# Softmax sums by 128x32 column tiles in one PSUM bank, spread by DMA, in a Linformer attention and max-out feed-forward kernel

## The chip, the cores and the metric

The kernel runs on one core of a Trainium2 chip. A core has a matrix engine (TensorE, PE in the profile), a vector engine (VectorE, DVE), a scalar engine for activations (ScalarE, ACT), GpSimd (POOL) and a sync engine (SP). Each takes its own instructions in order and waits on semaphores for the others. DMA transfers are issued from the queues of SP, POOL or ACT. TensorE writes to PSUM, which is used here as 8 banks of 128 partitions x 512 floats. The metric is the device time of one execution in microseconds; a kernel's time is the median of its runs.

## The reference

Batch 8, 8 heads, sequence 1024, head size 64, projection 64. The keys and values of each head are projected along the sequence, attention runs over the 64 projected rows, and the result goes through three parallel linear layers, of which the largest is kept, and an output layer.

```python
k_proj = np.einsum('ks,bhsd->bhkd', E, k)
v_proj = np.einsum('ks,bhsd->bhkd', F, v)
scores = scale * np.matmul(q, k_proj.transpose(0, 1, 3, 2))
scores = scores - np.max(scores, axis=-1, keepdims=True)
attn = np.exp(scores)
attn = attn / (np.sum(attn, axis=-1, keepdims=True) + 1e-09)
attn_out = np.matmul(attn, v_proj)
x = attn_out.transpose(0, 2, 1, 3).reshape(B * S, H * D)   # (8192, 512)
h = np.maximum(np.maximum(x @ w1, x @ w2), x @ w3)         # (8192, 768)
out = (h @ w_out).astype(np.float32)                       # (8192, 512)
```

The inputs are normal draws, q, k and v times 0.1.

## The kernel before

All matmuls are in bf16 with float sums. The feed-forward part of batch b and the attention of batch n = b + 1 are interleaved by hand on TensorE. The main loop goes over the batch steps b = 0 to 7, in each over two chunks of 512 tokens (`ch` 0 and 1), and in each chunk over ten steps. Steps 0 to 5 are `up` (one of six blocks of 128 hidden units): 3 weights x 4 matmuls of 128x512, a ScalarE copy of the first result (`h1s`, L566), and two VectorE maxima (`m12`, L570, and `hT`, L518). Steps 6 to 9 are `down` (one of four output steps of 128 tokens): 6 matmuls of 128x512, a copy to `o_sb` (L613 by L99, on ScalarE from batch step 1 on), and a store on SP's queue after every second one. The first `up` step of a chunk takes the last quarter of its input (`ct` 3) behind all else, so that the last head pair of `xT` may come late.

`plan(b)` says which pieces of attention follow which step. A key (ch, step) names the place: (1, 6) is behind the first output step of the second chunk. `behind` calls these pieces, and their instructions stand in each engine's queue in just that order; nothing reorders them. The pieces:

- `ld(b)` loads q, k, v of a batch from POOL's queue, cast to bf16 on the way. `k_t` and `v_t` have one buffer each, so a load waits until the projection has read the batch before.
- `qd(b)` is the turn of q: four VectorE copies to `q_p`, then a transposing DMA on SP's queue.
- `kproj`, `vproj`, `kt`: projections of k and v (128x64 tiles, L286) with their copies (v's by ScalarE, then by VectorE), and the turn of the projected k.
- `sc(b, g)`: scores of head pair g, four 64x64-tile matmuls into two banks (L202), and, later, the ScalarE exp to `pT` (L213). The exp is not emitted at once: `later` holds it until behind the next `h1s` or `o_sb` copy.
- `za(b, g)`: sums (L222 with `ones`) and values (L222 with `vp`), each four 64x64-tile matmuls into two banks by `pair_mm`. The matrix of ones puts the sum of the 64 exps into all 64 rows of a head, so that it stands beside the values. ScalarE takes the reciprocal as exp(-ln) in two passes (L235, L241) and VectorE multiplies (`scale_x`, L252), which gives `xT`.

Banks are dealt out when the program is built: `two()` takes the aligned pair, and `bank()` the one bank, that is free earliest by a rough clock in the program. On the chip an instruction of TensorE waits until the last reader of its bank is done, and all that stands behind it on TensorE waits too.

For batches 1 to 7 the pieces `sc` and `za` are spread over a batch step one pair at a time. Batch 0 has its own code, by half chunks, in front.

Of the kernel before, what the change touches and what calls it, by code (L numbers as in the profile page):

```python
# [8 lines left out]
FP32 = mybir.dt.float32  # L9
# [6 lines left out]
def kernel(  # L16
# [13 lines left out]
    nc = tc.nc  # L30
# [19 lines left out]
    const = ctx.enter_context(tc.tile_pool(name="const", bufs=1))  # L50
    loads = ctx.enter_context(tc.tile_pool(name="loads", bufs=1))
    att = ctx.enter_context(tc.tile_pool(name="att", bufs=2))
    psum = ctx.enter_context(tc.tile_pool(name="psum", bufs=1, space=bass.MemoryType.PSUM))

    ET = mybir.EngineType
# [23 lines left out]
    def bank():  # L79
        n = min(range(8), key=lambda n: free[n])  # L80
        deal((n,))
        return psum_t[:, n, :], (n,)
# [34 lines left out]

    ident = const.tile([P, P], BF16, name="ident")
    ones = const.tile([P, HALF], BF16, name="ones")
    warm = const.tile([P, 512], BF16, name="warm")  # L120
    warm_f = const.tile([P, 512], FP32, name="warm_f")
    w_sb = [const.tile([P, NCT, DF], BF16, name=f"w{i}_sb") for i in range(3)]
# [10 lines left out]
    def load_tiles(b):  # L133
        qkv[b] = tuple(
            loads.tile([P, H, SI, D], BF16, name=nm, bufs=n)
            for nm, n in (("q_t", 2), ("k_t", 1), ("v_t", 1))
        )
        return qkv[b]
# [33 lines left out]
    nc.vector.memset(warm, 0.0)  # L172
    make_identity(nc, ident)
    nc.vector.memset(ones, 1.0)

    load_w(0, slice(0, 2))
    load_kv(2, V2)
# [7 lines left out]
    load_w(2, slice(2, 4))  # L185
    nc.gpsimd.dma_start(out=wout_sb, in_=moe_w_out.rearrange("(jt p) m -> p jt m", p=P))

    def load(b):
        tiles = load_tiles(b)
        for i in range(3):  # L190
            dma = nc.gpsimd.dma_start(out=tiles[i], in_=view((q, k, v)[i], b))  # L191
            if i == 0 and b - 1 in last_T:
                after(dma, last_T[b - 1])
# [15 lines left out]

    def exps(b, g, lo, nsi, sc):  # L210
        t, ns, ready = sc
        pTs[b, g, lo] = att.tile([P, 2, CHUNK], BF16, name="pT", bufs=4)[:, :, 0:nsi * HALF]
        nc.scalar.activation(out=pTs[b, g, lo], in_=t, func=AF.Exp, scale=scale)  # L213
        runs("s", ready, 0.17 + nsi * 0.107, ns)

# [13 lines left out]
    def sums(b, g, lo, nsi):  # L229
        return pair_mm(b, g, lo, nsi, lambda rows, hp: ones[rows])  # L230

    def invert(b, g, lo, nsi, z):
        t, ns, ready = z
        zl = att.tile([P, 2, CHUNK], FP32, name="zl", bufs=1)[:, :, 0:nsi * HALF]
        nc.scalar.activation(out=zl, in_=t, func=AF.Ln)  # L235
        runs("s", ready, 0.17 + nsi * 0.107, ns)
        if nsi == SI:
            zi = att.tile([P, 2, CHUNK], FP32, name="zi", bufs=2)
        else:
            zi = att.tile([P, 2, CHUNK // 2], FP32, name="zi0", bufs=4)  # L240
        nc.scalar.activation(out=zi, in_=zl, func=AF.Exp, scale=-1.0)  # L241
        zis[b, g, lo] = zi, runs("s", ready, 0.17 + nsi * 0.107)
# [19 lines left out]
            f()  # L262
        later.clear()

    def sc(b, g, lo=0, nsi=SI):
        def f():
            t = scores(b, g, lo, nsi)
            later.append(lambda: exps(b, g, lo, nsi, t))
        return f

    def za(b, g, lo=0, nsi=SI, then=False):
        def f():
            z = sums(b, g, lo, nsi)
            av = values(b, g, lo, nsi)
            invert(b, g, lo, nsi, z)
            if then:
                later.append(lambda: scale_x(b, g, lo, nsi, av))
            else:
                scale_x(b, g, lo, nsi, av)
        return f  # L280
# [40 lines left out]
    def qd(b, parts=1):  # L321

        def f():
            q_p = att.tile([P, NPAIR, SI, 2, D], BF16, name="q_p", bufs=1)
            qTs[b] = att.tile([P, NPAIR * SI, P], BF16, name="qT")
            n = NPAIR // parts
            for lo in range(0, NPAIR, n):
                for g in range(lo, lo + n):
                    copy(
                        "v", q_p[:, g].rearrange("p si h d -> p h si d"),  # L330
                        qkv[b][0][:, 2 * g:2 * g + 2], (), 0.43,
                    )
                last_T[b] = nc.sync.dma_start_transpose(
                    out=qTs[b][:, lo * SI:(lo + n) * SI, :],
                    in_=q_p[:, lo:lo + n].rearrange("p g si h d -> p (g si h d)"),
                )
        return f

    kps = {}
    def kproj(b):  # L340
        def f():
            t, ns = bank()
            proj(b, 1, t, (LO, HI), 4 * D)
            kps[b] = att.tile([P, 2, 2 * D], BF16, name="kp")
            copy("v", kps[b].rearrange("a g x -> a (g x)"), t[:, 0:4 * D], ns, 0.43)
        return f
# [273 lines left out]

    def ld(b):
        return lambda: load(b)

    def plan(b):
        n = b + 1
        if b == 0:
            c1 = (SPC, SPC)
            return {  # L630
                (0, 6): [za(0, 1, *c1), sc(0, 3, *c1)],
                (0, 7): [qd(1, 2), za(0, 2, *c1)],
                (0, 8): [za(0, 3, *c1)],
                (1, 0): [kproj(1)],
                (1, 1): [kt(1)],
                (1, 2): [vproj(1), ld(2)],
                (1, (3, "mid")): [sc(1, 0), sc(1, 1)],
                (1, 4): [za(1, 0), sc(1, 2)],
                (1, 5): [za(1, 1), sc(1, 3)],
                (1, 7): [za(1, 2)],  # L640
                (1, 8): [za(1, 3)],
            }
        if b == 1:
            return {
                (0, 1): [qd(2)],
                (0, 5): [kproj(2), vproj(2), ld(3)],
                (0, 6): [kt(2)],
                (0, 7): [sc(2, 0)],
                (0, 9): [za(2, 0), sc(2, 1)],
                (1, 1): [za(2, 1), sc(2, 2)],  # L650
                (1, 3): [za(2, 2), sc(2, 3)],
                (1, 5): [za(2, 3)],
                (1, 6): [qd(3)],
            }
        if b == 2:
            return {
                (0, 2): [kproj(3), vproj(3), ld(4)],
                (0, 3): [kt(3)],
                (0, 4): [sc(3, 0)],
                (0, 6): [za(3, 0), sc(3, 1)],  # L660
                (1, 0): [za(3, 1), sc(3, 2), qd(4)],
                (1, 2): [za(3, 2), sc(3, 3), kproj(4), vproj(4), ld(5)],
                (1, 4): [kt(4)],
                (1, 5): [za(3, 3), sc(4, 0)],
            }
        if n == B:
            return {}
        out = {
            (0, 1): [za(n, 0), sc(n, 1)],
            (0, 3): [za(n, 1), sc(n, 2)],  # L670
            (0, 9): [za(n, 2), sc(n, 3)],
            (1, 3): [za(n, 3)],
        }
        if n + 1 < B:
            out[0, 6] = [qd(n + 1)]
            out[0, 9] += [kproj(n + 1), vproj(n + 1)]
            out[1, 1] = [kt(n + 1)]
            out[1, 3] += [sc(n + 1, 0)]
        if n + 2 < B:
            out[1, 1] += [ld(n + 2)]  # L680
        return out

    for b in range(B):
# [59 lines left out]
```

## Time and profile before

| what | value |
|---|---|
| median of 10 runs | 405.57 us (405.43 to 405.92) |
| the profiled execution | 405.4 us, span 403.4 us |
| granted TensorE clock | 1.00 |
| TensorE busy | 390.2 us |
| sums, values, scores (L222, L222, L202) | 144 matmuls each |
| ln (L235), exp(-) (L241), exp (L213) | 36 each, nearly all on 128x1024; 930, 962, 930 ns mean |
| batch steps 1 to 6 begin (first `up`) | 74.22, 122.19, 172.43, 219.66, 266.65, 313.65 us |
| batch step 7 begins | 358.39 us |

An engine's busy time counts its instructions' stretches; matmuls are pipelined and overlap, so their mean duration (379 ns for 128x512) is longer than the slot in which one follows another. The timeline gives each instruction, or run of equal ones, with its start and length in microseconds; in brackets stands the idle time of the engine before it and what ended it. "x23" where 24 were issued is a record missing in the trace.

### The profile page before, as it was taken

What the parts mean: (1) busy time and instruction counts of PE and PEld (TensorE: products, weight loads), DVE (VectorE), ACT (ScalarE), POOL (GpSimd) and SP (SyncE); (2) the same over time, 40 slices, a digit from 0 to 9 for tenths busy, and PEclk for the clock granted to TensorE, in tenths of its full rate; (3) what the DMA queues carried; (4) which work ended last, traced back from release to release, by engine and by line L of the source; (5) the groups of instructions that cost most, each with busy time, mean ns of one, the idle gap of its engine ahead of it and who ended that gap; (6) DMA issues with size and microseconds to landing.
All of it is one profiled execution on the core that took longest, in us unless ns stands there. A gap on an engine that the chain in (4) does not pass through costs nothing.

```text
span 403.4 us, 5831 instructions
## 1 busy us (share of the span) xinstructions
PE 390.2 (97%) x2309; PEld 178.4 (44%) x2351; DVE 203.4 (50%) x314; ACT 189.2 (47%) x274; POOL 31.6 (8%) x44
## 2 busy tenths in 40 slices
PE   6899999999999999999999999999999999999996
PEld 3444443444444435444544445444544444444443
DVE  2348755761764528437352655626364363525251
ACT  2622537525672376555643555437535555432322
POOL 7340001001000100200100002000000000000000
PEclk9999999999999999999999999999999999999999
DMA  9999999959908996893799039960510202020202
GB/s 150 206 205 208 231 202 163 242 124 187 225 2 215 190 222 106 127 237 54 211 177 213 27 32 220 202 173 0 152 59 2 104 2 104 0 106 0 106 0 105
DMA packets 62667, 53.33 MB, mean 132 GB/s; under 512 B 30128, under 2 KB 58288, under 8 KB 62640
## 3 DMA queue, kind: packets, MB, share of 16 engines
q0 software_dynamic: 28512, 28.31, 44.5%
q1 hardware_dynamic: 33984, 24.51, 20.7%
q8 instruction: 18, 0.29, 0.3%
q10 hardware_dynamic: 144, 0.13, 0.1%
q14 instruction: 9, 0.07, 0.1%
HBM read 57.15 MB, written 16.78 MB: 183 GB/s over the span
## 4 chain that ended last, share of the span: by engine, by line
PE 82%; DMA 11%; ACT 2%; DVE 1%; issue 1%; POOL 1%; DVEq 0%; ACTq 0%; POOLq 0%
PE banks L508 56%; PE banks L605 17%; DMA v_t<-in_v_dram 7%; PE banks L222 4%; DMA w_sb<-in_moe_w_dram 3%; PE banks L286 3%; PE banks L202 2%; ACT zi L241 1%; DVE xT L252 1%; ACT zl L235 1%; DMA out_dram<-o_sb 0%; POOL k_t L148 0%; POOL q_t L153 0%; POOL v_t L148 0%; DVE m L570 0%
## 5 line engine op out<-in xcount | busy, mean ns | idle before, releaser
L508 PE MATMUL banks<-xT,w_sb 128*128 128x512 bf16 x1120 | 255.0, 379 | 3.7 <-DMA w_sb<-in_moe_w_dram 1.3
L508 PEld LDWEIGHTS <-w_sb 128*128 128x128 bf16 x1152 | 109.5, 98 | 138.0 <-issue 10.6
L570 DVE TENSOR_TENSOR m<-banks,h1s 128x512 f32<-128x512 f32 x90 | 62.0, 689 | 85.1 <-ACT h1s L566 52.1
L566 ACT COPY h1s<-banks 128x512 f32<-128x512 f32 x90 | 52.4, 582 | 90.4 <-PE banks L508 88.3
L605 PE MATMUL banks<-wout_sb,hT 128*128 128x512 bf16 x369 | 84.6, 379 | 1.0 <-issue 0.6
L252 DVE TENSOR_TENSOR xT<-banks,zi 128x1024 bf16<-128x1024 f32 (+1 forms) x36 | 39.8, 1105 | 73.6 <-ACT zi L241 54.2
L518 DVE TENSOR_TENSOR hT<-banks,m 128x512 bf16<-128x512 f32 x90 | 62.3, 692 | 10.0 <-PE banks L508 0.8
L99 ACT COPY o_sb<-banks 128x512 f32<-128x512 f32 (+1 forms) x56 | 32.5, 581 | 52.5 <-PE banks L605 52.4
L605 PEld LDWEIGHTS <-hT 128*128 128x128 bf16 x378 | 35.9, 98 | 45.5 <-issue 3.1
L235 ACT ACTIVATE zl<-banks 128x1024 f32<-128x1024 f32 (+1 forms) x36 | 33.5, 930 | 31.4 <-PE banks L222 30.5
L213 ACT ACTIVATE pT<-banks 128x1024 bf16<-128x1024 f32 (+1 forms) x36 | 33.2, 930 | 15.4 <-PE banks L202 15.4
L241 ACT ACTIVATE zi<-zl 128x1024 f32<-128x1024 f32 (+1 forms) x36 | 34.6, 962 | 1.1
L191 POOL DMA_DIRECT2D q_t<-in_q_dram x7 | 6.1, 878 | 202.8 <-DMA qT<-q_p 64.1
L222 PE MATMUL banks<-pT,ones 64*64 64x512 bf16 (+1 forms) x144 | 13.7, 374 | 0.9 <-ACT pT L213 0.6
L222 PE MATMUL banks<-pT,vp 64*64 64x512 bf16 (+1 forms) x144 | 13.3, 355 | 0.4 <-DVE vp L99 0.4
L202 PE MATMUL banks<-qT,kpT 64*64 64x512 bf16 (+1 forms) x144 | 13.3, 358 | 0.3 <-DVE m L570 0.3
L286 PEld LDWEIGHTS <-efT 128*64 128x64 bf16 x224 | 11.6, 110 | 3.4 <-issue 2.7
L99 DVE CAST vp<-banks 64x256 bf16<-64x256 f32 (+1 forms) x18 | 7.1, 397 | 7.5 <-ACT vp L99 3.7
L222 PEld LDWEIGHTS <-ones 64*64 64x64 bf16 x144 | 4.4, 103 | 14.3 <-issue 14.2
L99 DVE COPY q_p<-q_t 128x1024 bf16<-128x1024 bf16 x28 | 10.0, 419 | 0.0
L99 ACT CAST vp<-banks 64x256 bf16<-64x256 f32 x14 | 5.1, 364 | 8.9 <-PE banks L286 8.7
L99 DVE COPY o_sb<-banks 128x512 f32<-128x512 f32 (+1 forms) x9 | 5.8, 653 | 4.5 <-DMA out_dram<-o_sb 4.5
(51 smaller groups left out, 105.1 us busy)
## 6 DMA issues: line engine op xcount, KB each, us to landing
out_dram<-o_sb SPq DMA_DIRECT2D x30, 512.0 KB, 3.2
q_t<-in_q_dram POOLq DMA_DIRECT2D x7, 1024.0 KB, 9.5
k_t<-in_k_dram POOLq DMA_DIRECT2D x7, 1024.0 KB, 13.8
v_t<-in_v_dram POOLq DMA_DIRECT2D x7, 1024.0 KB, 19.1
w_sb<-in_moe_w_dram POOLq DMA_DIRECT2D x5, 384.0 KB, 12.6
k_t<-in_k_dram POOLq DMA_DIRECT2D x2, 512.0 KB, 8.9
v_t<-in_v_dram POOLq DMA_DIRECT2D x4, 256.0 KB, 12.2
wout_sb<-in_moe_w_out_dram POOLq DMA_DIRECT2D x1, 768.0 KB, 15.6
```

Of the source, the lines that this page charges most:

```text
L99: done = {"v": nc.vector.tensor_copy, "s": nc.scalar.copy, "g": nc.gpsimd.tensor_copy}[eng](out=o, in_=i)
L213: nc.scalar.activation(out=pTs[b, g, lo], in_=t, func=AF.Exp, scale=scale)
L222: nc.tensor.matmul(out=t[hp * HALF:(hp + 1) * HALF, c, 0:nsi * HALF], lhsT=w(rows, hp), rhs=p[rows, hp, :], start=True, stop=True,)
L235: nc.scalar.activation(out=zl, in_=t, func=AF.Ln)
L241: nc.scalar.activation(out=zi, in_=zl, func=AF.Exp, scale=-1.0)
L252: nc.vector.tensor_tensor(out=xTs[b][:, g, lo:lo + nsi, :].rearrange("a (c s) p -> a c (s p)", c=2), in0=t, in1=zi, op=ALU.mult,)
L286: nc.tensor.matmul(out=t[hh * HALF:(hh + 1) * HALF, 0:width], lhsT=efT[:, si, (kv - 1) * KP:kv * KP], rhs=qkv[b][kv][:, heads[hh], si, :], ...
L508: nc.tensor.matmul(out=h, lhsT=w_sb[i][:, ct, jt * P:(jt + 1) * P], rhs=xTs[b][:, ct, ch * SPC:(ch + 1) * SPC, :], start=(ct == first), st ...
L518: nc.vector.tensor_tensor(out=o, in0=h, in1=other, op=ALU.max)
L566: nc.scalar.copy(out=h1s, in_=h[0][0])
L570: nc.vector.tensor_tensor(out=m12, in0=h[1][0], in1=h1s, op=ALU.max)
L605: nc.tensor.matmul(out=o_ps, lhsT=hTs[b, ch][:, jt, tt * P:(tt + 1) * P], rhs=wout_sb[:, jt, :], start=(jt == 0), stop=(jt == NJT - 1),)
```

## The change

- For batches 2 to 7 the sums no longer come from `za`. `zc(b)` makes all of a batch's sums in one bank: for each of four head pairs and two heads one matmul with a 128x32 weight `pick`, whose output goes to 32 partitions of its own (a column tile per pair; the second head is added to the first). `pick` has ones such that each sum fills eight rows. ScalarE takes ln and exp(-) of that one bank (128x512), every eighth row is stored to a scratch in DRAM (16 rows of 512 floats, SP's queue), and four DMAs of 512 KB bring it back, each row spread over 64 partitions, into `zi_all`, which has one buffer. These DMAs are on POOL's queue for batches 2, 3 and 4, on SP's from batch 5 on.
- The values of these batches are a piece of their own, `vx`, behind it.
- Scores are put together: four pairs at one place (`scs`), the first three exps at once instead of through `later`. `pT` has six buffers instead of four.
- Batch 1 keeps `za`, but its last two pairs follow at one place, (1, 7).
- The plan is new: the turn of q, projections, loads and scores of a batch have other places; for batch 4 and 5 the load of v is apart from that of q and k.

```diff
+    def zc(b, queue=nc.sync):
+        def f():
+            t, ns = bank()
+            for hp in range(2):
+                for g in range(NPAIR):
+                    nc.tensor.matmul(
+                        out=t[32 * g:32 * (g + 1), :], lhsT=pick[:, hp, :],
+                        rhs=pTs[b, g, 0][:, hp, :], start=(hp == 0), stop=(hp == 1),
+                    )
...
+            nc.scalar.activation(out=zlc, in_=t, func=AF.Ln)
...
+            nc.scalar.activation(out=zic, in_=zlc, func=AF.Exp, scale=-1.0)
...
+            nc.sync.dma_start(
+                out=zd.rearrange("g h c f -> (g h c) f"),
+                in_=zic.rearrange("(a r) f -> a r f", r=8)[:, 0, :],
+            )
+            for u in range(2):
+                gs = slice(2 * u, 2 * u + 2)
+                for hp in range(2):
+                    queue.dma_start(
+                        out=zi_all(b)[hp * HALF:(hp + 1) * HALF, gs],
+                        in_=zd[gs, hp].partition_broadcast(HALF),
+                    )
...
+    def vx(b, g):
+        def f():
+            scale_x(b, g, 0, SI, values(b, g, 0, SI))
+        return f
...
-                (1, 7): [za(1, 2)],
-                (1, 8): [za(1, 3)],
+                (1, 7): [za(1, 2), za(1, 3)],
             }
+        def scs(n):
+            return [sc(n, g, now=(g < NPAIR - 1)) for g in range(NPAIR)]
+
+        def vxs(n, gs):
+            return [vx(n, g) for g in gs]
+
         if b == 1:
             return {
-                (0, 1): [qd(2)],
-                (0, 5): [kproj(2), vproj(2), ld(3)],
-                (0, 6): [kt(2)],
-                (0, 7): [sc(2, 0)],
-                (0, 9): [za(2, 0), sc(2, 1)],
-                (1, 1): [za(2, 1), sc(2, 2)],
-                (1, 3): [za(2, 2), sc(2, 3)],
-                (1, 5): [za(2, 3)],
-                (1, 6): [qd(3)],
+                (0, 0): [qd(2)],
+                (0, 3): [kproj(2), vproj(2)],
+                (0, 4): [kt(2)],
+                (0, 5): scs(2),
+                (0, 7): [zc(2, nc.gpsimd), ld(3)],
+                (1, 3): vxs(2, (0, 1)),
+                (1, 6): vxs(2, (2, 3)),
+                (1, 7): [qd(3)],
             }
         if b == 2:
             return {
-                (0, 2): [kproj(3), vproj(3), ld(4)],
-                (0, 3): [kt(3)],
-                (0, 4): [sc(3, 0)],
-                (0, 6): [za(3, 0), sc(3, 1)],
-                (1, 0): [za(3, 1), sc(3, 2), qd(4)],
-                (1, 2): [za(3, 2), sc(3, 3), kproj(4), vproj(4), ld(5)],
-                (1, 4): [kt(4)],
-                (1, 5): [za(3, 3), sc(4, 0)],
+                (0, 3): [kproj(3), vproj(3), ld(4, (0, 1))],
+                (0, 4): [kt(3)],
+                (0, 6): scs(3),
+                (0, 8): [zc(3, nc.gpsimd), ld(4, (2,))],
+                (0, 9): [qd(4)],
+                (1, 6): [kproj(4)] + vxs(3, range(NPAIR)),
+                (1, 7): [kt(4), ld(5, (0, 1))],
             }
         if n == B:
             return {}
-        out = {
-            (0, 1): [za(n, 0), sc(n, 1)],
-            (0, 3): [za(n, 1), sc(n, 2)],
-            (0, 9): [za(n, 2), sc(n, 3)],
-            (1, 3): [za(n, 3)],
-        }
-        if n + 1 < B:
-            out[0, 6] = [qd(n + 1)]
-            out[0, 9] += [kproj(n + 1), vproj(n + 1)]
-            out[1, 1] = [kt(n + 1)]
-            out[1, 3] += [sc(n + 1, 0)]
+        out = {(0, 3): [zc(n)]}
+        if n == 4:
+            out[0, 1] = scs(n)
+            out[0, 3] = [zc(n, nc.gpsimd), vproj(n), ld(n + 1, (2,))]
+        if n + 1 == B:
+            out[1, 6] = vxs(n, range(NPAIR))
+            return out
+        out[0, 4] = [qd(n + 1)]
+        out[1, 2] = [kproj(n + 1), vproj(n + 1)] + vxs(n, (0, 1, 2))
+        out[1, 3] = [kt(n + 1)]
+        out[1, 6] = scs(n + 1)
+        out[1, 6][1:1] = vxs(n, (3,))
         if n + 2 < B:
-            out[1, 1] += [ld(n + 2)]
+            out[1, 3] += [ld(n + 2)]
         return out
```

## The prediction

> **What bounds the kernel.** I read the page's shares first, then the chain, then who waited for whom on TensorE, then the timeline around one attention step.
>
> ```profile
> PE 390.2 (97%) x2309; PEld 178.4 (44%) x2351; DVE 203.4 (50%) x314; ACT 189.2 (47%) x274; POOL 31.6 (8%) x44
> PE 82%; DMA 11%; ACT 2%; DVE 1%; issue 1%; POOL 1%; DVEq 0%; ACTq 0%; POOLq 0%
> PE banks L222 <- DVE xT L252: 0.3, 1, 0.3
> 318.92 0.41 PE L222 MATMUL banks<-pT,ones 64*64 64x512 bf16 x4
> 319.16 0.39 PE L222 MATMUL banks<-pT,vp 64*64 64x512 bf16 x4
> 319.38 0.39 PE L202 MATMUL banks<-qT,kpT 64*64 64x512 bf16 x4
> 319.70 5.35 PE L508 MATMUL banks<-xT,w_sb 128*128 128x512 bf16 x23
> 324.98 0.41 PE L222 MATMUL banks<-pT,ones 64*64 64x512 bf16 x4
> ```
>
> TensorE is the bound: 97% busy, and the waits listed for it are tenths. So the time changes by what TensorE no longer executes, minus what it newly waits for; ScalarE and VectorE (half idle) matter only through when they free a bank. The five timeline lines give prices. From 318.92 to 324.98 is 6.06 us: 24 large matmuls of 0.216 (the chain has "5.18, x24") and three groups of four 64x64 matmuls. A group lasts 0.213 (319.16 to 319.38), so 6.06 - 5.18 - 0.64 = 0.24 us is the price of one visit to the tiled mode, in and out.
>
> The other prices, from the timeline:
>
> ```profile
> 59.23 1.94 ACT L213 ACTIVATE pT<-banks 128x1024 bf16<-128x1024 f32 x2 [0.63 <-PE banks L202]
> 65.49 1.22 DVE L252 TENSOR_TENSOR xT<-banks,zi 128x1024 bf16<-128x1024 f32 x1 [1.81 <-ACT zi L241]
> 66.63 0.68 DVE L570 TENSOR_TENSOR m<-banks,h1s 128x512 f32<-128x512 f32 x1
> 66.77 0.41 PE L222 MATMUL banks<-pT,ones 64*64 64x512 bf16 x4 [0.35 <-DVE xT L252]
> 290.00 1.06 PE L286 MATMUL banks<-k_t,efT 128*64 128x256 bf16 x16
> 291.87 5.42 PE L508 MATMUL banks<-xT,w_sb 128*128 128x512 bf16 x23
> 291.97 0.74 ACT L99 CAST vp<-banks 64x256 bf16<-64x256 f32 x2
> 308.47 5.34 PE L605 MATMUL banks<-wout_sb,hT 128*128 128x512 bf16 x24
> 309.97 0.58 ACT L99 COPY o_sb<-banks 128x512 f32<-128x512 f32 x1 [2.44 <-PE banks L605]
> ```
>
> An exp takes 1.03, the next starts 0.91 after it. A scaling of a pair takes 1.22, the next starts 1.14 later. The first output step's six matmuls end their slots at 308.47 + 1.30 = 309.77 and its copy starts at 309.97: a consumer starts 0.20 after the last slot. VectorE ends at 66.71, TensorE goes on at 66.77: a released bank is used 0.05 later. The two projections take 1.87; ScalarE's half of the vp copies follows until 292.71, VectorE's (0.87) only then.
>
> **The change, part by part.** All offsets below are from the program's bank allotment in the changed order and these rows.
>
> 1. Sums. Six batches (2 to 7) lose 4 groups of sums: -24 x 0.213 = -5.11. They gain eight 128x32 column matmuls in two rounds of four. Before has no such tile. Bounds: four at a time 2 x 0.213 = 0.43, one at a time 8 x 0.216 = 1.73. Nearest row: the 128x64 projections, 32 matmuls of 256 columns in 1.87, 0.058 each against 0.108 for 256 columns alone, so pairs do run together. I take 0.43: +2.56. Net -2.55.
>
> The page "TensorE: Matmul & The Clock Gate" (Measured speedup vs the span model) has three 32-column tiles at 2.38 times, not 3. An estimate from it for four is 3.17 times, 0.54 us a batch instead of 0.43, which would make the sum 0.7 us longer; no row of this trace shows it.
>
> 2. Visits. By the order, batch steps 1 to 6 have 5, 5, 4, 4, 4, 4 visits before and 4, 3, 4, 3, 3, 2 after: 7 fewer, -1.68. (One more is lost in batch step 0, in point 4.)
>
> 3. ScalarE loses 8 passes of 0.93-0.96 a batch and gets two of 128x512 (copies of that size 0.58): nothing directly, it has idle time. Old waits end with it. Batch steps 1, 2, 3 last 47.97, 50.24, 47.23; their content by these prices is 47.2, 49.4, 47.0. Less the 0.33 that belongs to point 4: -1.5 if all of it goes, 0 if none; I take -1.5.
>
> 4. Batch step 0: the last two sum-and-value pairs now follow at once. The second's values need the bank of the first's sums, free when its Ln ends (71.95); 0.9 us of waiting, then two output steps and nine matmuls end at 76.85, where before the last third goes on at 76.49. +0.36.
>
> 5. Groups put together. TensorE takes instructions in order, and one pair takes two of eight banks, so whoever is fourth waits, and everything queued behind it.
> - (1,6) of steps 3, 4, 5: score, value, three scores after an output step (end = 0). The output's copy runs 0.20 to 0.78, the first exp 0.66 to 1.69, and the fourth score group has the first one's banks: it starts at 1.74 instead of 0.95. 0.78 each, 2.34.
> - (1,2) of the same steps: both projections and three values. VectorE does the vp copies until 3.63, scalings until 4.79, 5.93, 7.07. The next up step starts at 2.72; its second, third bank and the k turn wait for the vp copy, the first and the second scaling: 0.10 + 0.29 + 0.28 = 0.67 each, 2.01.
> - Four scores at once: step 1 (0,5) 0.53, step 2 (0,6) 0.68, step 3 (0,1) 0.53: the following matmul's bank waits for the first exp.
> - The new sums in steps 1 and 2 come two output steps later; the fourth exp (which now queues behind an output copy) ends at 4.74 and 4.9, 0.4 and 0.35 after they could go.
> - Four values: step 2 (1,6), after the k projection, 0.74; step 6 0.72: the next output waits for the first scaling.
> Sum 8.3. Bounds: each of these 13 places as short as the longest bank wait of before (0.35) is 4.6; with the 0.20 from slot end to consumer counted twice at each it is 10.9. I take 8.3, because every piece is a row of the same instruction.
>
> The page "TensorEngine Tiling" (PSUM Bottleneck) says the same in general: tiling makes TensorE faster, not the emptying of PSUM. It gives no price.
>
> 6. DMA. Six 32 KB stores on SP (an output store of 128 KB lands in 2.0 us) and 24 broadcasts of 512 KB. The store waits on SP for ScalarE's second pass, with output stores and the q turn queued behind it. For batches 2, 3, 4 the broadcasts wait on POOL for the store (issue 0.88 each), with load(3), v of 4 and v of 5 queued behind; for batches 5 to 7 they wait on SP, ahead of the q turn and output stores, which have over 10 us to spare. Broadcast speed is between output stores (0.11 of 47 us for 2 MB: 1.3 us each) and the casting loads (44.5% of 403.4 us for 28.3 MB: 3.2 each); their 4 KB float rows are the output stores', so I take 1.3. Then v(3) lands near 128 and is needed near 134, v(5) near 201 against 204.5. At 3.2 each they are late by about 1 and 3.5 us, directly on TensorE. The reciprocals come 6 us or more before their scalings (batch 2 has the least: first pair near 104.5, scaling near 111). Taken: 0. Batch 2's projections two steps earlier: k lands at 74.2 (60.38 + 13.8), v at 81.05, needed at 85. The q turns' four DVE copies (1.42) move two steps forward, beside work. Five small memsets of pick at the start lie before the data comes.
>
> Sum against the profiled execution's own 405.4 (span 403.4 and 2.0 around it): -2.55 - 1.68 - 1.5 + 0.36 + 8.3 = +2.9, so 408.3; the median stands 0.17 above that execution: 408.5.
>
> **Rivals.**
> - The waits cost no more than bank waits do now. For it: TensorE's list before shows no wait for a bank over 0.35. Against: before never asks for more than three pairs at once. At 0.35 each the sum is -0.8, 404.7. The point is 5.4 us of new waits; below it the change gains.
> - The broadcasts run like casting loads: 4.5 us later, 413. For it: DMA at 9 in many slices up to 225 us. Against: row size.
> - The column tiles run two at a time, or one: +2.6 or +7.8, so 411 or 416. The 64-wide pairs speak against it.
> - Gains and waits cancel: 405 to 406.3.
>
> **How the numbers follow.** Forecast 0.56 (own range 406.5 to 410.5: 8.3 by a quarter either way); broadcasts or tiles 0.16; waits short 0.19; cancel 0.09. Within 0.2% (0.8 us) is what a measurement of this kernel can't tell from no change. So slower 0.72, same 0.09, faster 0.19. The range 404.3 to 412.0 takes in the short waits and reaches to the first tile case, leaving out a tenth on either side.
>
> **What would show it.** Right: TensorE waits of 0.7 to 0.8 for pT and xT at (1,6), 0.1 to 0.3 for vp and xT after the projections, 1.0 to 1.5 us in total per batch step 3 to 5, each 0.7 to 1.2 longer than the 47.0 of before; step 6 about 1 shorter than 44.8; a sums visit of 0.6 to 0.7. Wrong: steps 4 and 5 at 46.5 or below (waits absent), a sums visit over 1 us, or projections waiting for v_t.

## The result, and the profile after

The changed kernel takes 413.39 us (median of 8 runs, 412.67 to 414.60) against 405.60 us of the kernel before (28 runs beside them): a ratio of 1.0194, 95% interval 1.0185 to 1.0204. It is 7.8 us slower. The forecast was 408.5 us with a range to 412.0: the sign was right, the size was not, and the time lies outside the range. The profiled execution took 412.7 us, span 410.9 us, mean granted clock 0.995. Times of the experiments are medians of four to twelve runs; one of these runs, at a granted clock of 0.949, fell in a slower state of the chip and is left out.

The page of the changed kernel has these lines for the shares and the chain, then for the DMA queues (q0 carries GpSimd's transfers, q1 SP's) and the bytes moved over the span:

```profile
PE 391.7 (95%) x2261; PEld 179.3 (44%) x2303; DVE 203.5 (50%) x319; ACT 148.9 (36%) x238; POOL 39.0 (9%) x56
PE 75%; DMA 13%; ACT 4%; DVE 3%; issue 2%; POOL 1%; DVEq 0%; ACTq 0%; POOLq 0%
q0 software_dynamic: 30240, 34.61, 49.8%
q1 hardware_dynamic: 35904, 31.00, 29.4%
HBM read 69.73 MB, written 16.97 MB: 211 GB/s over the span
```

48 matmul records fewer are in it (24 groups of four less, 48 column tiles more, no others changed), ScalarE lost 40 us, and yet TensorE is idle for more of the span. The chain runs over DMA for 13% instead of 11%. From the list of who TensorE waited for (in all, times, longest):

```profile
PE banks L345 <- DMA v_t<-in_v_dram: 3.2, 2, 3.1
PE banks L211 <- ACT pT L222: 1.5, 3, 0.5
PE banks L664 <- DVE xT L308: 1.3, 2, 0.7
PE banks L664 <- ACT pT L222: 0.8, 2, 0.5
PE banks L567 <- DVE xT L308: 0.4, 2, 0.2
PE banks L256 <- ACT pT L222: 0.3, 2, 0.2
```

Line 345 is the projections, 211 the scores, 256 the new sums, 567 `up`, 664 `down`. The last five lines are the bank and exp waits of point 5. The first is a transfer, which the prediction had counted at nothing. To see which of the two made the 7.8 us, the length of each batch step (from its first `up` to that of the next) is set beside the kernel before. The last column is an experiment, told below, in which no transfer of batch step 3 is late:

| batch step | before | changed | changed, broadcasts of batch 4 on SP |
|---|---|---|---|
| 1 | 47.97 | 47.67 | 47.66 |
| 2 | 50.24 | 49.41 | 49.41 |
| 3 | 47.23 | 54.62 | 50.53 |
| 4 | 46.99 | 47.90 | 47.90 |
| 5 | 47.00 | 47.90 | 47.91 |
| 6 | 44.74 | 43.93 | 43.92 |
| sum | 284.17 | 291.43 | 287.33 |

Steps 4 and 5 are 0.9 longer and step 6 is 0.8 shorter, as forecast (0.7 to 1.2, and about 1). One step is not: step 3. There the timeline of the changed kernel's TensorE reads (start, length, engine, line, and in brackets the idle time before and what ended it):

```profile
203.58 1.06 PE L345 MATMUL banks<-k_t,efT 128*64 128x256 bf16 x16
207.72 1.06 PE L345 MATMUL banks<-v_t,efT 128*64 128x256 bf16 x16 [3.07 <-DMA v_t<-in_v_dram]
208.71 1.49 PE L231 MATMUL banks<-pT,vp 64*64 64x512 bf16 x12
210.54 3.31 PE L567 MATMUL banks<-xT,w_sb 128*128 128x512 bf16 x11 [0.34 <-issue]
```

The projection of v stands 4.14 us behind that of k instead of 0.90: 3.24 us are lost to the load of v for batch 5. The three values behind it then take 1.83 us to the next `up` where the experiment's take 1.00: 0.83 more. Together 4.07 of the 4.09 us by which step 3 is too long. Why the values are slow is in the windows over these microseconds (stretch, its length, busy time of each engine, granted clock, DMA share, GB/s):

```profile
201.00:205.00 4.00, 3.64 (x29) 1.78 (x26) 2.39 (x4) 0.59 (x1) 0.00 (x0) 1.00 1.21 195
205.00:208.00 3.00, 0.28 (x6) 0.29 (x8) 0.11 (x1) 0.00 (x0) 0.00 (x0) 1.00 1.34 137
208.00:212.00 4.00, 3.67 (x32) 1.62 (x28) 2.36 (x4) 0.73 (x2) 1.51 (x2) 0.59 1.15 375
208.70:209.60 0.90, 0.90 (x14) 0.37 (x12) 0.00 (x1) 0.73 (x2) 0.00 (x0) 0.50 1.27 290
209.60:210.50 0.90, 0.60 (x8) 0.13 (x2) 0.85 (x3) 0.00 (x0) 0.01 (x1) 0.50 1.12 445
```

After the pause the granted clock is 0.59 over 4 us, and 0.50 over the values (the last two lines). And the DMA share is above 1 all through: the 16 engines had transfers in flight in every one of these stretches. What they carried is in the changed kernel's transfers, each asked for singly (KB, us from issue to landing; the broadcasts here are the one issued at 188.0 and, last, the one at 189.9):

```profile
zi_all<-zd POOLq DMA_DIRECT2D x1, 512.0 KB, 4.9
...
zi_all<-zd POOLq DMA_DIRECT2D x1, 512.0 KB, 10.2
...
v_t<-in_v_dram POOLq DMA_DIRECT2D x1, 1024.0 KB, 17.2
qT<-q_p SPq DMA_TRANSPOSE x1, 20.0
```

So the four broadcasts land from 192.9 to 200.1, about 2.4 us apart. The load of v, issued behind them on GpSimd's queue at 190.50, needs 17.2 us, and the turn of q, issued on SP at 190.22, needs 20. In the kernel before, the same turn ran with no load beside it. First the line of SP's queue from the kernel before, then that of the changed kernel:

```profile
192.02 4.10 SPq L333 DMA_TRANSPOSE qT<-q_p  x1
```

```profile
190.22 17.96 SPq L392 DMA_TRANSPOSE qT<-q_p  x1
```

The 2.4 us are the broadcasts' own. Those for batch 7, issued from 336.37 to 338.2 with no load and no turn beside them, land about as far apart; the first and the last of them:

```profile
zi_all<-zd SPq DMA_DIRECT2D x1, 512.0 KB, 5.0
...
zi_all<-zd SPq DMA_DIRECT2D x1, 512.0 KB, 10.1
```

Three theories follow. The queue: v is late because it is issued behind the broadcasts. The engines: broadcasts, load and turn share the same time, whatever their order. And, for the rest, that the bank waits of point 5 cost what they were priced at.

### The profile page after: what moved, and what is told of

Read it like the earlier page. It is cut to its first block, busy times and chain, and to the rows that moved or that the text cites. A ratio compares the mean times of both kernels' runs of the same rounds, so it can differ in the third digit from the quotient of the medians.

```text
span 410.9 us, 5751 instructions
## 1 busy us (share of the span) xinstructions
PE 391.7 (95%) x2261; PEld 179.3 (44%) x2303; DVE 203.5 (50%) x319; ACT 148.9 (36%) x238; POOL 39.0 (9%) x56
## 4 chain that ended last, share of the span: by engine, by line
PE 75%; DMA 13%; ACT 4%; DVE 3%; issue 2%; POOL 1%; DVEq 0%; ACTq 0%; POOLq 0%
PE banks L567 51%; PE banks L664 16%; DMA v_t<-in_v_dram 11%; PE banks L345 3%; ACT pT L222 3%; DVE xT L308 3%; PE banks L231 2%; DMA k_t<-in_k_dram 2%; PE banks L256 1%; ACT zl L291 1%; PE banks L211 1%; DVE vp L102 1%; PE banks L470 0%; POOL zi_all L275 0%; PE banks L496 0%
## 5 line engine op out<-in xcount | busy, mean ns | idle before, releaser
L222 ACT ACTIVATE pT<-banks 128x1024 bf16<-128x1024 f32 (+1 forms) x36 | 32.0, 935 | 18.1 <-PE banks L211 18.1
L308 DVE TENSOR_TENSOR xT<-banks,zi_all 128x1024 bf16<-128x1024 f32 x28 | 33.1, 1219 | 10.9 <-PE banks L231 5.4
L345 PEld LDWEIGHTS <-efT 128*64 128x64 bf16 x224 | 11.5, 110 | 7.3 <-DMA v_t<-in_v_dram 4.0
L275 POOL DMA_DIRECT2D zi_all<-zd x12 | 7.3, 620 | 76.0 <-DMA zd<-zic 39.6
L211 PE MATMUL banks<-qT,kpT 64*64 64x512 bf16 (+1 forms) x144 | 12.0, 364 | 1.6 <-ACT pT L222 1.5
L231 PE MATMUL banks<-pT,vp 64*64 64x512 bf16 (+1 forms) x144 | 11.7, 382 | 1.2 <-ACT zl L291 0.8
L291 ACT ACTIVATE zl<-banks 128x512 f32<-128x512 f32 (+1 forms) x12 | 8.9, 739 | 5.2 <-PE banks L231 4.4
L345 PE MATMUL banks<-v_t,efT 128*64 128x256 bf16 x112 | 7.4, 274 | 3.2 <-DMA v_t<-in_v_dram 3.2
L211 PEld LDWEIGHTS <-kpT 64*64 64x64 bf16 x144 | 4.5, 104 | 9.2 <-issue 6.8
L441 PE MATMUL banks<-warm_f 128*128 128x512 f32 x8 | 6.6, 977 | 1.5 <-DVE warm_f L175 1.5
```

What stands on the lines that cost most here:

```text
L211: nc.tensor.matmul(out=t[c * HALF:(c + 1) * HALF, hp, 0:n * P], lhsT=kpTs[b][rows, g, :], rhs=qTs[b][rows, at:at + n, :], start=True, stop ...
L231: nc.tensor.matmul(out=t[hp * HALF:(hp + 1) * HALF, c, 0:nsi * HALF], lhsT=w(rows, hp), rhs=p[rows, hp, :], start=True, stop=True,)
L308: nc.vector.tensor_tensor(out=xTs[b][:, g, lo:lo + nsi, :].rearrange("a (c s) p -> a c (s p)", c=2), in0=t, in1=zi, op=ALU.mult,)
L345: nc.tensor.matmul(out=t[hh * HALF:(hh + 1) * HALF, 0:width], lhsT=efT[:, si, (kv - 1) * KP:kv * KP], rhs=qkv[b][kv][:, heads[hh], si, :], ...
```

## The experiments

### Which queue, and in which order

Two kernels with the same work in batch step 3. In one the load of v goes ahead of the broadcasts:

```diff
-            out[0, 3] = [zc(n, nc.gpsimd), vproj(n), ld(n + 1, (2,))]
+            out[0, 3] = [vproj(n), ld(n + 1, (2,)), zc(n, nc.gpsimd)]
```

> Edit: in batch step 3 the projection of v and the load of v for batch 5 stand ahead of the sums and their broadcasts; all else is as in the changed kernel. Theory A (v of batch 5 comes late because it stands on POOL's queue behind four broadcasts of 512 KB: 17.2 us from issue to landing against 9.4 for a first load alone; the wait of 3.07 us on TensorE then drops its clock, 0.59 granted in the 4 us behind it): the wait and the clock dip go, batch step 3 falls from 54.6 to about 50.4, the whole to 408.3 to 409.3 us (-4.2 to -5). Rival R1 (the DMA engines are simply loaded too much by broadcasts, loads and the q turn at once, whatever the order): v still lands at about 207, the time stays within 1 us of 413.4.

In the other the broadcasts go to SP's queue, so that neither stands behind the other:

```diff
-            out[0, 3] = [zc(n, nc.gpsimd), vproj(n), ld(n + 1, (2,))]
+            out[0, 3] = [zc(n), vproj(n), ld(n + 1, (2,))]
```

> Edit: the broadcasts of batch 4 are issued from SP instead of POOL, behind the same store; the load of v of batch 5 is no longer behind them on POOL but runs on the DMA engines beside them. Theory A (the place on POOL's queue): v lands 9.5 to 12 us after an issue at about 185, no wait, 408.5 to 409.5 us. Rival R1 (shared engines): broadcasts and load slow each other as before, v lands near 200 to 207 and the wait stays in part, 411 to 413.4 us.

With v first the time hardly moved: 413.51 us (410.77 to 414.89), ratio 1.0186 (1.0146 to 1.0226). v landed 9.6 us after its issue and nobody waited for it. But the 32 KB store of the reciprocals, 1.8 us in the changed kernel, took 6.0 beside it. So the broadcasts were issued at 194.38 instead of 188.03 and ran beside the turn of q. First the line of GpSimd's queue, then that of TensorE:

```profile
194.38 2.36 POOL L275 DMA_DIRECT2D zi_all<-zd  x4 [7.48 <-DMA zd<-zic]
```

```profile
215.03 5.18 PE L567 MATMUL banks<-xT,w_sb 128*128 128x512 bf16 x16 [2.44 <-DVE xT L308]
```

The wait moved from v to a scaling that lacks its reciprocals, with a dip of the clock behind it again (0.85, then 0.72 in the two windows of 4 us from 212). With this order it is another transfer that comes late.

With the broadcasts on SP the time is 409.56 us (408.97 to 409.80), ratio 1.0095 (1.0080 to 1.0110). v is issued at 186.38, ahead of the broadcasts, and they at 188.35; the store, issued at 186.42, takes 1.8 us here. v lands 15.7 us after its issue, at 202.1, and is needed at 205.2:

```profile
204.26 1.07 PE L345 MATMUL banks<-k_t,efT 128*64 128x256 bf16 x16
205.16 1.04 PE L345 MATMUL banks<-v_t,efT 128*64 128x256 bf16 x16
```

No transfer is late and the clock stays at 1.00. The 409.56 is what the changed kernel takes without its DMA wait, and lies 1.1 us from the forecast, which had that wait at zero. Each theory came in part: v landed as late as shared engines would have it, and yet in time. The page "DMA: Bandwidth & Descriptors" of the Trainium skill (Issuing engines are not separate DMA queues) says that transfers started by any engine run on the same 16 DMA engines and interleave. The runs agree: on another queue than the broadcasts, v took 15.7 us, and 9.6 where they came later.

### The bank waits

Both kernels of this pair stand on the one with v first. In one the four scores of (1, 6) are parted:

```diff
-        out[1, 6] = scs(n + 1)
-        out[1, 6][1:1] = vxs(n, (3,))
+        four = scs(n + 1)
+        out[1, 6], out[1, 7] = [four[0], *vxs(n, (3,)), four[1]], four[2:]
```

> Edit: e1_v_first, and in batch steps 3 to 5 the four scores behind (1,6) are parted: two with the value pair behind (1,6), two behind (1,7). Theory A (the fourth group waits for the first exp, 0.78 us a batch step, one more visit costs 0.24): steps 4 and 5 fall by 0.5 to 0.55 each, in all 1.5 to 1.7 below e1_v_first. Rival R2 (the longer batch steps come from the new kind of tile and its mode changes, not from banks): 0.7 above e1_v_first for three more visits.

In the other the values of (1, 2) go ahead of the projections:

```diff
-        out[1, 2] = [kproj(n + 1), vproj(n + 1)] + vxs(n, (0, 1, 2))
+        out[1, 2] = vxs(n, (0, 1, 2)) + [kproj(n + 1), vproj(n + 1)]
```

> Edit: e1_v_first, and behind (1,2) of batch steps 3 to 5 the three value pairs stand ahead of the two projections instead of behind them. The work and the number of visits are the same. Theory A (the scalings stand behind the vp copies on VectorE and hold the banks, 0.67 us a batch step): the waits for vp and xT there go, steps 4 and 5 fall by 0.5 to 0.7 each, in all 1.5 to 2.0 below e1_v_first. Rival R2: no difference, within 0.3 us.

Their medians, 411.17 us (ratio 1.0133, 1.0104 to 1.0162) and 412.22 us (1.0188, 1.0140 to 1.0236), say little, since both carry the late reciprocals of batch step 3, which differ from run to run. In the second they show as two waits:

```profile
208.73 2.75 PE L567 MATMUL banks<-xT,w_sb 128*128 128x512 bf16 x11 [1.05 <-DVE xT L308]
214.08 0.28 PE L412 MATMUL banks<-ident,kp 128*128 128x128 bf16 x2 [2.60 <-DVE kp L102]
```

The undisturbed steps 4 and 5 decide. They last 47.33 and 47.33 us with the scores parted, 47.09 and 47.09 with the values first, 47.90 without either. Parting gives 0.57 (0.78 of waiting less a visit of 0.24 makes 0.54). The values first give 0.81, more than the 0.67 that was priced. Both waits are real, they sit where point 5 put them, and they go when the order goes.

### Who shares the engines with the load of v

Back to the changed kernel's own order. First, half the bytes in the broadcasts, by reciprocals that are rounded to bf16 (the output changes by that rounding):

```diff
-            zi_alls[b] = att.tile([P, NPAIR, 2, CHUNK], FP32, name="zi_all", bufs=1)
+            zi_alls[b] = att.tile([P, NPAIR, 2, CHUNK], BF16, name="zi_all", bufs=1)
...
-            zic = att.tile([P, CHUNK], FP32, name="zic", bufs=1)
+            zic = att.tile([P, CHUNK], BF16, name="zic", bufs=1)
...
-            zd = scratch.tile([NPAIR, 2, 2, CHUNK], FP32, name="zd")
+            zd = scratch.tile([NPAIR, 2, 2, CHUNK], BF16, name="zd")
```

> The order of the changed kernel, but the reciprocals are kept, stored and spread in bf16 (they are rounded to bf16, the output differs by that): the broadcasts move 256 KB each instead of 512 KB, with the same number of rows. Theory A (what is short in batch step 3 is bytes on the shared DMA engines): the load of v for batch 5, still issued near 190.5, lands by 204.5 instead of 207.7, TensorE does not wait for it, batch step 3 lasts about 50.5 us as with the broadcasts on SP, median 409 to 410 us. Theory B (the engines are held per row, whatever its length): the load still lands 16 to 17 us after its issue, the wait stays at 2.5 to 3 us, batch step 3 lasts 54 to 55 us, median 413 us. Steps 4 and 5 (47.9) and 6 (43.9) stay by both.

The median is 411.43 us (409.92 to 414.40), ratio 1.0151 (1.0117 to 1.0184), 2.0 below the changed kernel's. It was mixed: two of the four runs were near 410 with a clock of 1.00, one at 412.5, and the profiled one was the longest, 414.4. In that one the broadcasts did land about 1.2 us apart, the last 5.4 us after its issue, at 196.0 instead of 200.1. Yet v gained nothing. The line of TensorE, then that of SP's queue:

```profile
208.24 1.92 PE L345 MATMUL banks<-v_t,efT 128*64 128x256 bf16 x16 [2.94 <-DMA v_t<-in_v_dram]
```

```profile
203.00 1.08 SPq L678 DMA_DIRECT2D out_dram<-o_sb  x2
```

From 196.0 on v had the turn of q beside it, from 203.00 on also two output stores that the turn had held back, and took 12.2 us more. So in this run neither theory of the expectation holds as written: the broadcasts are paid by their bytes, but that is not all that holds v. The two runs near 410 have about the time that the theory of bytes gave; no trace of them was kept. Next, float broadcasts again, and the turn of q eight microseconds later:

```diff
-        out[0, 4] = [qd(n + 1)]
+        out[(1, 0) if n == 4 else (0, 4)] = [qd(n + 1)]
```

> The changed kernel, float reciprocals and broadcasts on GpSimd's queue ahead of the load of v as in it; only the turn of q for batch 5 in batch step 3 is moved from (0, 4) to (1, 0), some 8 us later. With bf16 reciprocals, half the bytes, the load of v still took 17.0 us and the turn of q 19.6, so the bytes of the broadcasts are not what holds it. Theory C (the transposing DMA of q, with its thousands of packets under 512 B, and the load of v hold each other up on the same engines): v, issued near 190.5, lands before 203.5, TensorE does not wait for it, the turn takes under 12 us to land, batch step 3 lasts 50.5 us and the median is 409 to 410 us. Theory B (the broadcasts ahead of it on GpSimd's queue hold the load, by their rows): v lands near 207.5 as before, batch step 3 lasts 54 us, median 413 us.

It became worse, 415.23 us (414.39 to 418.71), ratio 1.0263 (1.0209 to 1.0316). v landed 18.4 us after its issue. In its profile the waiting instruction and SP's queue read:

```profile
210.53 1.92 PE L345 MATMUL banks<-v_t,efT 128*64 128x256 bf16 x16 [4.21 <-DMA v_t<-in_v_dram]
```

```profile
195.60 2.92 SPq L678 DMA_DIRECT2D out_dram<-o_sb  x2
203.25 8.55 SPq L392 DMA_TRANSPOSE qT<-q_p  x1
```

The broadcasts land by 201.8, as their price says, v 8.7 us after them. With the turn gone, two output stores of 512 KB, which in the changed kernel stood behind it on SP until 208.27, run at 195.60 beside the broadcasts. So the turn is not the one culprit either. If the engines' time simply adds up, both edits together must do what neither did in its profile:

> Both edits that did nothing alone: bf16 reciprocals (half the bytes of the broadcasts, the output rounded accordingly) and the turn of q for batch 5 at (1, 0) instead of (0, 4). In the runs so far the four broadcasts land one after another, 2.4 us apart in float (192.9, 195.5, 197.9, 200.3) and 1.2 apart in bf16 (192.5, 193.7, 195.0, 196.2), and the load of v behind them lands 7.4 to 12.0 us after the last. Theory E (the engines' time adds up, whoever uses it: v is behind the broadcasts in its queue and shares with what SP sends, so that one edit alone only lets the other in): the last broadcast lands 4.6 us sooner than with the later turn alone, v lands 13 to 14 us after its issue and TensorE waits for it 0.5 us at most; batch step 3 lasts 50.5 to 51.5 us, median 409 to 410.5 us. Rival (a load queued behind broadcasts takes 17 us for another reason, whatever the others move): v lands 17 us after its issue, the wait is 3 us or more, median 412 us or more.

410.20 us (three runs, 409.61 to 410.65), ratio 1.0112 (1.0091 to 1.0132). TensorE waits 0.85 us instead of 3.07:

```profile
206.01 1.06 PE L345 MATMUL banks<-v_t,efT 128*64 128x256 bf16 x16 [0.85 <-DMA v_t<-in_v_dram]
```

v lands 15.1 us after its issue, the turn of q 7.4 after its own, and batch step 3 lasts 51.54. The direction is what the sum of the engines' time gives, and the rival (17 us whatever the others move) falls. But v came 1 to 2 us later than expected and the wait is a little over the 0.5 allowed. And the three runs are no shorter than the two short ones with bf16 alone (410.42 and 409.92). So what each neighbour takes, the turn of q above all, was not measured.

### The waits taken away

If bank waits and late transfers are all that the change costs, the work that it removes must show once they are gone. First both edits of (1, 2) and (1, 6) on the kernel with the broadcasts on SP:

> The changed kernel with its broadcasts for batch 4 on SP, the scores at (1, 6) parted into (1, 6) and (1, 7), and at (1, 2) the values ahead of the projections. Measured alone, parting took 0.57 us from each of batch steps 4 and 5 (47.90 to 47.33), and the values first 0.81 (to 47.09). Theory A (both are bank waits of different places, which add up): steps 4 and 5 last 46.5, step 3 about 49.1, median 409.6 - 3 x 1.38 = 405.4 us, level with the kernel before. Rival (one wait takes the place of the other, as the exps or copies are then late elsewhere): steps 4 and 5 last 47.0 to 47.1 and the median is 407 us.

405.04 us (404.75 to 406.81), ratio 0.9986 (0.9977 to 0.9995). Steps 4 and 5 last 46.52 and 46.51: the two gains add up, and these steps are now shorter than the 47.0 of before. The content says by how much: 4 groups of 0.213 less, two rounds of column tiles of 0.213 more, the same four visits, 0.43 in all; measured 0.48. The profiled run is the longest of the twelve, 406.81; in it step 2 lasts 50.98, with 1.41 us of waiting for a scaling at its end.

Then the other places parted too, and every broadcast on SP:

```diff
-                (1, 7): [za(1, 2), za(1, 3)],
+                (1, 7): [za(1, 2)],
+                (1, 8): [za(1, 3)],
...
-            return [sc(n, g, now=(g < NPAIR - 1)) for g in range(NPAIR)]
+            return [sc(n, g, now=True) for g in range(NPAIR)]
...
-                (0, 5): scs(2),
-                (0, 7): [zc(2, nc.gpsimd), ld(3)],
+                (0, 5): scs(2)[:2],
+                (0, 6): scs(2)[2:],
+                (0, 8): [zc(2), ld(3)],
...
-                (0, 6): scs(3),
-                (0, 8): [zc(3, nc.gpsimd), ld(4, (2,))],
+                (0, 5): scs(3)[:2],
+                (0, 6): scs(3)[2:],
+                (0, 8): [zc(3), ld(4, (2,))],
...
-                (1, 6): [kproj(4)] + vxs(3, range(NPAIR)),
-                (1, 7): [kt(4), ld(5, (0, 1))],
+                (1, 5): vxs(3, (0, 1)),
+                (1, 6): [kproj(4)],
+                (1, 7): [kt(4), ld(5, (0, 1))] + vxs(3, (2, 3)),
...
-            out[0, 1] = scs(n)
+            out[0, 1], out[0, 2] = scs(n)[:2], scs(n)[2:]
...
-            out[1, 6] = vxs(n, range(NPAIR))
+            out[1, 5], out[1, 7] = vxs(n, (0, 1)), vxs(n, (2, 3))
```

> The kernel of the run before this one, with all broadcasts on SP and the other places where pairs were put together parted too: the last sums and values of batch 1 an output step apart as before the change (0.36 less in step 0), scores two and two in batch steps 1, 2 and 3 with all four exps at once, the sums an output step later in step 1 (0.93 less but one visit of 0.24 more; 1.03 less and 0.24 more in step 2; 0.53 less and 0.24 more in step 3), values two and two in steps 2 and 6 (0.74 and 0.72 less, 0.24 more each). Theory A (these waits are as priced, and the work that the change removes comes through once they are gone): 3.2 us below the run before, 402 us, with step 0 ending near 74.2, step 1 at 47.0, step 2 at 48.1, step 6 at 43.4. Rival (the waits move to the next place, or the DMA engines are late earlier): 404.5 to 406 us, with a wait for v_t or xT in steps 1 to 3.

404.93 us (404.29 to 406.45), ratio 0.9988 (0.9977 to 0.9998): the rival's time, and only in step 1. Steps 2 to 6 last 48.03, 48.84, 46.52, 46.51 and 43.42 us, where the terms gave 48.1, about 48.8, 46.5, 46.5 and 43.4. Step 1 lasts 50.26 instead of 47.0. There the store of the reciprocals and the broadcasts of batch 2 now run beside the loads for batch 3. The store takes 5.7 us, the broadcasts, issued from 106.55 on, land 6.9 to 11.5 us after their issues, and the values at (1, 3) lack them:

```profile
117.17 1.89 PE L567 MATMUL banks<-xT,w_sb 128*128 128x512 bf16 x7 [1.82 <-DVE xT L308]
121.09 0.39 PE L664 MATMUL banks<-wout_sb,hT 128*128 128x512 bf16 x1 [0.96 <-DVE hT L577]
```

The last run gives them time, by a later place and not by another queue:

```diff
-                (1, 3): vxs(2, (0, 1)),
-                (1, 6): vxs(2, (2, 3)),
-                (1, 7): [qd(3)],
+                (1, 5): vxs(2, (0, 1)),
+                (1, 6): [qd(3)],
+                (1, 7): vxs(2, (2, 3)),
```

> The kernel with all groups parted, but in batch step 1 the values of batch 2 stand at (1, 5) and (1, 7) instead of (1, 3) and (1, 6), and the turn of q for batch 3 between them, at (1, 6): there the reciprocals landed 9.3 us after their issue at 106.6, and TensorE waited 2.8 us. In that kernel steps 2 to 6 lasted 48.0, 48.8, 46.5, 46.5 and 43.4 us, all within 0.1 of what the terms gave; step 1 alone was long (50.3 instead of 47.0). Theory A (the late reciprocals are the whole of it): step 1 lasts 47.0 to 47.2 and the median is 404.9 - 3.2 = 402 us. Rival (on a DMA that is busy from 100 to 118 us the transfer that moves later makes another late, the turn of q or the loads for step 2): step 2 grows by 1 us or more and the median stays above 403.5 us.

401.48 us (401.27 to 402.25) against 405.13: ratio 0.9908 (0.9893 to 0.9923). Step 1 lasts 47.15, step 2 48.04. This kernel is faster than both. Its page, and its list of TensorE's waits, in which the longest inside a batch step is 0.5:

```profile
PE 391.8 (98%) x2303; PEld 176.3 (44%) x2303; DVE 203.2 (51%) x319; ACT 148.5 (37%) x238; POOL 31.5 (8%) x44
```

```profile
PE banks L345 <- DMA v_t<-in_v_dram: 0.5, 1, 0.5
PE banks L231 <- DVE vp L102: 0.4, 2, 0.2
PE banks L231 <- DVE xT L308: 0.3, 1, 0.3
PE banks L567 <- DVE xT L308: 0.2, 1, 0.2
```

Steps 1 to 6 last 280.46 us in all, 3.7 less than before the change. The 7.8 us that the change lost were order and place: with the same new sums the kernel gains.

## Why the prediction was wrong

**Points 1 and 2, the sums and the visits.** Right. The visit for the new sums in batch step 4 of the changed kernel:

```profile
236.73 0.62 PE L256 MATMUL banks<-pT,pick 128*32 128x512 bf16 x8
237.28 5.35 PE L567 MATMUL banks<-xT,w_sb 128*128 128x512 bf16 x24
```

Step 4 begins at 226.28 and 48 matmuls of 0.216 end their slots at 226.28 + 10.37 = 236.65; the next `up` starts at 237.28. That is 0.63 against the forecast 0.43 + 0.24 = 0.67. The column tiles run four at a time, and the rivals with two or one are out. So is the estimate that the prediction drew from the page "TensorE: Matmul & The Clock Gate" (0.54 instead of 0.43, so 0.78 for the visit).

**Point 4, batch step 0.** Right in size, but not to be read from where step 1 begins. That it begins at 74.58 instead of 74.22, just 0.36 later, is luck: other runs with the same batch step 0 begin step 1 at 75.11 to 76.32. It shows from the sums of pair 2 on. In the kernel before:

```profile
70.40 0.41 PE L222 MATMUL banks<-pT,ones 64*64 64x512 bf16 x4
76.49 3.83 PE L508 MATMUL banks<-xT,w_sb 128*128 128x512 bf16 x16 [0.16 <-DVE xT L252]
```

In the changed kernel:

```profile
70.05 0.41 PE L231 MATMUL banks<-pT,ones 64*64 64x512 bf16 x4
74.58 5.77 PE L567 MATMUL banks<-xT,w_sb 128*128 128x512 bf16 x25
```

Before, 6.09 us pass until the last third of the first `up`. Now nine matmuls of 0.216 end at 76.52, 6.47 after the sums: 0.38 more. It is 0.71 more up to the start of step 1, and 0.33 less behind it, where the wait ahead of the last third is gone.

**Point 5, the groups put together.** Right in place and nearly in size. In batch step 4 of the changed kernel the scores at (1, 6) read:

```profile
268.73 0.70 PE L211 MATMUL banks<-qT,kpT 64*64 64x512 bf16 x8
269.94 0.41 PE L211 MATMUL banks<-qT,kpT 64*64 64x512 bf16 x4 [0.52 <-ACT pT L222]
```

Two groups start at 268.73 and 0.213 later, so the fourth group could start at 269.16, and starts at 269.94: 0.78 late, as forecast. (The bracket has 0.52, since the ends of matmuls are modelled.) The four values in steps 2 and 6 have 0.68 and 0.59 in the brackets. Counted by slots, the next output starts 0.89 behind the last of them in both; 0.14 of that is the way out (the output behind the scores above starts 0.35 after a group of 0.21), so the wait is 0.75 where 0.74 and 0.72 were forecast.

**Points 1 to 5 together, and point 3.** The forecast has +2.2 for them over batch steps 1 to 6: 2.9 less the 0.69 by which point 4 delays the start of step 1 (its 0.36, and the 0.33 that it gives back in step 1). The kernel without the DMA wait measures 287.33 - 284.17 = +3.2, so 0.9 more. The values behind the projections, 0.81 each instead of 0.67, are 0.4 of that. The rest lies in steps 1 and 2: by the prediction's prices and the moved pieces they would last 47.5 and 49.1 us, and last 47.67 and 49.41. That old waits of 1.5 us all end there, as point 3 took it, was not tested on its own and seems too much.

**Point 6, DMA, "Taken: 0".** This is the step that failed, at three places.

- The price of a broadcast. The prediction chose 1.3 us each "since their 4 KB float rows are the output stores'". They measured 2.4, in batch 7 with no load beside them too, over half way to the 3.2 of casting loads that was kept as the other end. By the prediction's own count, four of them at 2.4 bring v from 201 to 205.4, 0.9 late. For v(3) the same count gives 132.4, and it landed at 132.0, in time.
- The turn of q. Of its move the prediction counted the four VectorE copies "beside work". It did not count the DMA that the move issues, though that ran at 192.02 with no load beside it before and now meets the broadcasts and the load of v. The load landed at 207.7, 2.3 us later than the price of the broadcasts explains. The profiles point to neighbours on the engines whose time adds up: with half the broadcasts v has the turn and the stores beside it, with the later turn it has broadcasts and stores, and with both edits the wait falls from 3.07 to 0.85. How the 2.3 us divide among them stays open.
- The clock. The prediction counted a late transfer "directly on TensorE", microsecond for microsecond. The 0.83 that the lower clock cost behind the pause was in no step.

3.24 + 0.83 = 4.07 us. The profiled execution's span grew by 7.5 us, 4.6 more than the 2.9 of the forecast: 4.1 from this step and 0.9 from points 3 and 5, less 0.35 by which this execution came sooner to the sums in batch step 0, and 0.1 behind the start of step 7. The median of the changed kernel lies 0.7 above this execution.

The rival "the broadcasts run like casting loads" gave 413 and had the mechanism that came: a projection that waits for `v_t`, which the last paragraph of the prediction had named as the sign of a wrong forecast. It had the time nearly right by errors that cancel, since it put the price too high and left the turn and the clock out. Nor is its own sum right: four broadcasts at 1.9 more put v(3) 1.6 and v(5) 4.1 us late by its landing times, which makes 414 and not 413, and v(3) was not late at all. Where it failed most is in the weight: "For it: DMA at 9 in many slices up to 225 us" is a statement about the very resource that the change loads with 12 MB more, and it was set against one argument, row size.

## What to carry to other kernels

A moved step moves its transfers too: before pricing a DMA at nothing, write down, for the stretch in which it runs, every transfer that any queue has in flight there, add up how long each takes alone as a first estimate, and compare the sum with the time to the first consumer. Where that is tight, the order in the queues decides who is late. A good order can leave nobody late with the same bytes, as the broadcasts on SP did in batch step 3; where none is found, a later consumer helps, as in batch step 1. And work that stands grouped on TensorE costs a wait for banks that could here be read off beforehand to within 0.15 us a place, so a saving by a cheaper form is to be judged only with its groups parted.

## What the runs showed of the hardware

- The granted clock falls behind a pause of TensorE. In the profiles with a pause of 3.07, 2.94 and 4.21 us for v it was 0.59, 0.50 and 0.57 over the 4 us from 208, 208 and 210 us; with 2.44 us (v first) it was 0.85 and then 0.72 over the 4 us from 212 and from 216. In shorter windows it is 0.50 at the lowest in all four. With a pause of 2.60 (values first) and of 0.85 it stayed at 1.00. The page "TensorE: Matmul & The Clock Gate" (Why this matters for your kernels) sets the bound near 3 us. Here 2.44 was too long once and 2.60 was not, so a bound between cannot be told from these runs.
- The transposing DMA of q, 4.10 us on its queue and 7.3 to landing with no load or broadcast beside it, took 17.96 and 20.0 beside four broadcasts and a load. In the changed kernel, SP's output stores stood behind it until 208.27.
- A store of 32 KB, 1.8 us to landing in the changed kernel, took 6.0 us when a casting load of 1 MB had been issued 1.8 us before it (v first), and 1.8 us when the load had been issued only 0.04 us before (broadcasts on SP).
- Broadcasts of 64 copies of 4 KB rows land 2.4 us apart for 512 KB, and 1.2 apart for 256 KB in rows of 2 KB: paid by bytes, not by rows. With no load beside them (batch 7) the 512 KB land as far apart.
